# A gated feed-forward after window attention on one core: the first product in a seven-product Strassen form from the sixth chunk on

## The chip, the cores and the metric

The kernel runs on one core of one Trainium2 chip. The metric is the device time of one execution in microseconds; smaller is better. Five engines work side by side, each with its own queue of instructions in a fixed order: PE (TensorE, the matmuls, with weight loads shown as PEld), DVE (VectorE), ACT (ScalarE), POOL (GpSimd), and SP, whose queue issues all transfers. Semaphores tie them together.

## The reference

Sliding-window attention over 8 batches, 8 heads, 576 positions with heads of 64, then a feed-forward with a gate on all 4608 tokens:

```python
scores = scale * np.matmul(q, k.transpose(0, 1, 3, 2))
mask = (rel >= 0) & (rel < window)          # rel = query - key, window = 64
scores = np.where(mask, scores, -1000000000.0)
attn = softmax(scores)
x = (attn @ v)                              # tokens x 512
h = x @ w_in                                # 512 -> 2048
sp = np.maximum(h, 0.0) + np.log1p(np.exp(-np.abs(h)))
g = h * erf(sp)
out = g @ w_out                             # 2048 -> 512
```

The weights come as 64-bit floats and are rebuilt on the chip to 32 bits and then to pairs of f16 numbers.

## The kernel before

**Tiling.** The 4608 tokens are worked in 36 units of 128 tokens for the attention (`u` in the code) and 18 chunks of 256 tokens for the feed-forward (`c`). Each chunk is split into two halves of the hidden dimension (1024 each); a chunk and a half make one of 36 groups (`g`).

**Precision.** Every f32 operand of a matmul is split into a high f16 and a low f16 part, and a product is made of three matmuls: high by high, high by low, low by high. So `x` becomes `xs[0]`, `xs[1]` (`x_hi`, `x_lo`), and after a transposing transfer (`x_turn`) `xt[0]`, `xt[1]`; the weights are `w1[0]`, `w1[1]` and `w2[0]`, `w2[1]`; the gated hidden values are `ghb`, `glb` (`g_hi`, `g_lo`).

**The first product.** `mm1(g, pc)` (L573) makes one of four pieces of a group's hidden values. A piece is 256 hidden features by 256 tokens: 2 feature blocks, 4 blocks of the 512 input features, 3 terms, so 24 matmuls with 128x128 weights and 256 columns, all into one of two banks of PSUM (`hps`, called hp in the profile). `hidden` (L585) then drains the bank, scaled, into `hb` in SBUF, on ACT or DVE. The next piece but one needs that bank again.

**The gate.** On each half of a group (128x1024), ACT makes softplus and erf (L593, L597; each change of function costs a table load), DVE multiplies (`gate`, L601), ACT or DVE casts to gh (`g_hi`), DVE makes gl (`g_lo`, L327 in `rest`). `yb` holds four halves.

**The second product.** `mm2` (L610) makes 16 matmuls of 512 columns with gh (`mA`) and 8 with gl (`mB`) for each half of a group, into two banks `ops`. `result` drains them into `ob`, `store` sends it out.

**The order.** There is no scheduler at work: a long string `PLAN` lists tokens such as `mm:30:1`, `ev:30:1:v` or `gh:29:1:a` (name, numbers, engine letter), and a loop calls the handler of each in turn. The order of the tokens is the order on every engine, the queue SP included. The engine letter says who does a pass: `a` ACT, `v` DVE, `g` POOL. The tokens of the attention of a later chunk (`s` scores, `m` masked maximum, `f` shift, `e` exponential, `a` weighting, `n` normalizing) stand between those of the feed-forward of an earlier one. The listing of the changed kernel numbers its lines anew: `product` is L673 there, `add` L689, the copy in `take` L472 on ACT and L474 on DVE, `mm2` L730.

Of the kernel before, what the change touches and what calls it, by code (L numbers as in the profile page):

```python
# [702 lines left out]
```

## Time and profile before

| | |
|---|---|
| time, median of 3 runs | 900.38 us (898.97 to 901.08) |
| the profiled execution | 900.86 us, its span 899.0 us |
| first product, L581 | 3456 matmuls of 256 columns |
| second product, L617 | 1728 matmuls of 512 columns |
| HBM read, written | 59.44 MB, 9.44 MB |
| largest part of the chain that ended last | PE, 68% |

In the lines of the profile the numbers after a bar are the busy time, the mean duration of one instruction in ns, and then the idle time of the engine just before these instructions with what ended it. A matmul's duration runs from its entry to its last result, and neighbours overlap; how fast matmuls follow each other is read from their start times.

### The profile page before, as it was taken

Reading aid. Unit: us, or ns where it says so; the run is one execution under the profiler, and the core shown is the slowest. Engines: PE = TensorE matmul, PEld = TensorE weight load, DVE = VectorE, ACT = ScalarE, POOL = GpSimd, SP = SyncE. Lnnn points to the kernel's source line nnn. Section 1 sums busy time; section 2 is a strip of 40 time slices with the busy share of each in tenths; the row PEclk is TensorE's granted clock in tenths of the full one; section 3 lists DMA queues with packets and bytes.
Section 4 is the critical chain, followed back from the end, with each engine's and each line's share of the span. In section 5 each row is a group of like instructions: output and inputs, shape, how many; then the busy total and the mean of one; then the engine's idle time right before and its main releaser. Section 6 shows DMA issues by size and latency. Waiting matters only on the chain.

```text
span 899.0 us, 21735 instructions
## 1 busy us (share of the span) xinstructions
PE 866.0 (96%) x9025; PEld 588.4 (65%) x9025; DVE 707.7 (79%) x1594; ACT 701.9 (78%) x814; POOL 192.4 (21%) x195
## 2 busy tenths in 40 slices
...
GB/s 359 305 203 139 203 184 120 71 153 42 51 97 134 131 126 59 137 84 135 89 121 98 141 91 106 65 89 113 118 107 95 63 106 57 49 48 42 7 24 23
DMA packets 140530, 98.59 MB, mean 110 GB/s; under 512 B 117776, under 2 KB 117904, under 8 KB 140432
## 3 DMA queue, kind: packets, MB, share of 16 engines
...
HBM read 59.44 MB, written 9.44 MB: 77 GB/s over the span
## 4 chain that ended last, share of the span: by engine, by line
PE 68%; ACT 13%; DVE 8%; DMA 8%; issue 2%; SPq 0%; POOL 0%; ACTq 0%; DVEq 0%; POOLq 0%
PE o L617 34%; PE hp L581 30%; DMA qr<-q_in 4%; PE av L434 2%; PE s L399 2%; DMA vr<-v_in 2%; ACT L597 1%; ACT y L597 1%; ACT y L593 1%; ACT sm L417 1%; ACT h L320 1%; ACT L593 1%; ACT gh L320 1%; ACT junk L345 1%; ACT L417 1%
## 5 line engine op out<-in xcount | busy, mean ns | idle before, releaser
L581 PE MATMUL hp<-xt,w 128*128 128x256 f16 x3456 | 396.2, 273 | 3.6 <-ACT h L320 1.7
L581 PEld LDWEIGHTS <-w 128*128 128x128 f16 x3456 | 335.9, 98 | 64.0 <-issue 5.3
L617 PE MATMUL o<-w,gh 128*128 128x512 f16 x1152 | 260.6, 379 | 2.9 <-ACT gh L320 2.2
L617 PEld LDWEIGHTS <-gh 128*128 128x128 f16 x1152 | 110.7, 98 | 126.6 <-ACT gh L320 2.7
L617 PE MATMUL o<-w,gl 128*128 128x512 f16 x576 | 136.2, 379 | 0.0
L601 DVE TENSOR_TENSOR y<-h,y 128x1024 f32<-128x1024 f32 x72 | 92.1, 1282 | 38.6 <-ACT y L597 38.3
L320 ACT ACTIVATE h<-hp,c 128x512 f32<-128x512 f32 x85 | 57.6, 678 | 68.7 <-PE hp L581 61.9
L327 DVE SCALAR_TENSOR_TENSOR gl<-y,sg,gh 128x1024 f16<-128x1024 f32 x72 | 94.0, 1307 | 16.6 <-PE o L617 7.9
L593 ACT ACT_TABLE_LOAD x68 | 87.2, 1283 | 21.5 <-DVE h L322 16.9
L617 PEld LDWEIGHTS <-gl 128*128 128x128 f16 x576 | 54.8, 98 | 55.5
L597 ACT ACT_TABLE_LOAD x68 | 87.2, 1283 | 1.2
L413 POOL TENSOR_TENSOR sm<-sm,mx 128x512 f32<-128x512 f32 x41 | 51.3, 1257 | 172.2 <-DVE mx L408 144.2
L593 ACT ACTIVATE y<-h 128x1024 f32<-128x1024 f32 x72 | 75.9, 1056 | 9.6 <-DVE h L322 8.9
L597 ACT ACTIVATE y<-y 128x1024 f32<-128x1024 f32 x72 | 75.9, 1057 | 0.8
L322 DVE TENSOR_SCALAR h<-hp,c 128x512 f32<-128x512 f32 x59 | 43.9, 745 | 40.1 <-PE hp L581 39.2
L408 DVE CUSTOM_DVE_ANT_0 sm<-s,mask 128x128 f32<-128x128 f32 x288 | 64.6, 284 | 7.1 <-PE s L399 6.7
L417 ACT ACTIVATE sm<-sm,shift,cde 128x512 f32<-128x512 f32 x72 | 57.2, 810 | 13.5 <-POOL sm L413 9.4
L320 ACT ACTIVATE gh<-y,sg 128x1024 f16<-128x1024 f32 x44 | 50.0, 1139 | 16.6 <-DVE y L601 8.5
L424 POOL TENSOR_TENSOR p<-sm,p 128x512 f16<-128x512 f32 x32 | 42.5, 1330 | 52.2 <-ACT p L449 29.0
L327 DVE SCALAR_TENSOR_TENSOR vs<-vr,csc,vs 128x1024 f16<-128x1024 f32 x36 | 48.7, 1355 | 1.0 <-ACT vs L320 0.8
L459 POOL TENSOR_TENSOR xs<-x,xs 128x512 f16<-128x512 f32 x17 | 27.0, 1586 | 104.6 <-DVE xs L451 69.0
L417 ACT ACT_TABLE_LOAD x36 | 46.2, 1283 | 0.6
...
## 6 DMA issues: line engine op xcount, KB each, us to landing
...
```

What stands on the lines that cost most here:

```text
L320: nc.scalar.activation(dst, src, AF.Copy, scale=s)
L322: nc.vector.tensor_scalar(dst, src, s, None, op0=ALU.mult)
L327: nc.vector.scalar_tensor_tensor(dst, src, s, hi, op0=ALU.mult, op1=ALU.subtract)
L408: nc.vector.tensor_tensor_reduce(smi(u, par)[:, j, :], sps[par][:, j, :], mask[:, var, :], 1.0, LOWEST, op0=ALU.add, op1=ALU.max, accum_ou ...
L413: eng_of(eng).tensor_tensor(s, s, m.unsqueeze(2).broadcast_to([P, HP, P]), op=ALU.subtract)
L417: nc.scalar.activation(s, s, AF.Exp, bias=shift14, scale=es)
L424: eng_of(eng).tensor_tensor(pp[1][u % 2][:, sl, :], smi(u, par), pp[0][u % 2][:, sl, :], op=ALU.subtract)
L581: nc.tensor.matmul(hps[pc % 2][:, f, :], w1[a][:, cc, fs], xt[b][c % 2][:, cc, :], start=(n == 0), stop=(n == 3 * NCC - 1))
L593: nc.scalar.activation(at(yb, g, n), at(hb, g, n), AF.Softplus)
L597: nc.scalar.activation(y, y, AF.Erf)
L601: nc.vector.tensor_tensor(y, at(hb, g, n), y, op=ALU.mult)
L617: nc.tensor.matmul(ops[j], a[:, f, ts], w2[b][:, hf * GF + f, :], start=f == 0 and a is gh and b == 0, stop=f == GF - 1 and a is gl)
```

## The change

From the sixth chunk on (`FAST = 5`, groups 10 to 35) the four pieces of a group's first product are replaced by seven products in a seven-product form of Strassen's algorithm. The two halves that a matrix is cut into are: the 512 input features in two of 256, the hidden features of a 512-wide block in two of 256, and the 256 tokens in two of 128. A product is `product(g, m)`: 24 matmuls with 128x128 weights and 128 columns. Three products start a bank, four add to what a bank holds; between them the banks are copied into `hb` (`take`, four times) or added to what is there (`add`, three times, on DVE).

The sums of weights that the form needs are made once on the chip, in f32 in `tmp`, and split into two f16 parts (`w_sums`, tokens `S`); they live in three tiles `stage` that held raw weights before, and the fourth sum overwrites a block of `w1`. The sums of x are made for each chunk (`x_sums`, tokens `xd`) in `xo`, so the second unit of a chunk splits and transposes 1280 columns instead of 512.

Scaling moves: `hb` is no longer scaled when drained; softplus takes a scale, the gate multiplies by one, and from the sixth chunk on gh and gl are a plain cast and a plain subtraction, so that gl may run on POOL. `yb` holds three halves instead of four. The string `PLAN` is new as a whole; softplus and erf stand more often in pairs in it.

On PE, the end of one piece and the start of the next in a late group of the kernel before (`w_0` and `w_1` are the high and low parts of w_in, `xt` the transposed x, `hp` the two banks, `gh` with `o` is the second product):

```order
L617 MATMUL o_156<-w_1_140,gh 128x512
L581 LDWEIGHTS w_0_137
L581 MATMUL hp_153<-xt_0_133,w_0_137 128x256
L581 LDWEIGHTS w_0_137
L581 MATMUL hp_153<-xt_0_135,w_0_137 128x256
L581 LDWEIGHTS w_1_138
L581 MATMUL hp_153<-xt_0_133,w_1_138 128x256
```

The same engine in the changed kernel, where the second product of group 33 ends and the sixth begins (`stage` holds sums of weights):

```order
L673 MATMUL hp_155<-xt_0_134,w_0_136 128x128
L673 LDWEIGHTS w_1_137
L673 MATMUL hp_155<-xt_0_132,w_1_137 128x128
L673 LDWEIGHTS stage_149
L673 MATMUL hp_154<-xt_0_132,stage_149 128x128 [waits Activation_49]
L673 LDWEIGHTS stage_149
L673 MATMUL hp_154<-xt_0_134,stage_149 128x128
```

Each matmul has half the columns and still its own weight load, and a product that adds to a bank waits for ACT, which copied the bank out.

On DVE, the last stretch of the kernel before (`h` is `hb`, `c` its scale, `y` is `yb`, `ob` the result):

```order
L322 TENSOR_SCALAR h_142<-hp_153,c_89 128x512 [waits PE_49,Activation_49]
L601 TENSOR_TENSOR y_144<-h_142,y_144 128x1024 [waits Activation_49]
L322 TENSOR_SCALAR gh<-y_144,sg 128x1024 [waits DVE_49]
L327 SCALAR_TENSOR_TENSOR gl<-y_144,sg,gh 128x1024 [waits DVE_49]
L322 TENSOR_SCALAR ob_147<-o_155,sg 128x512 [waits DMAHW6_49,PE_49]
L601 TENSOR_TENSOR y_144<-h_142,y_144 128x1024 [waits Activation_49]
```

And in the changed one, some ten rows from its end:

```order
L689 TENSOR_TENSOR h_140<-hp_155,h_140 128x2x2x128 [waits DVE_49,PE_49]
L721 TENSOR_TENSOR gl<-y_143,gh 128x1024 [waits Activation_49]
L689 TENSOR_TENSOR h_140<-hp_154,h_140 128x2x2x128 [waits Activation_49]
L689 TENSOR_TENSOR h_140<-hp_155,h_140 128x2x2x128 [waits PE_49]
L689 TENSOR_TENSOR h_141<-hp_155,h_141 128x2x2x128 [waits PE_49,Activation_49]
L707 SCALAR_TENSOR_TENSOR y_142<-h_140,cy,y_142 128x1024 [waits DVE_49,Activation_49]
```

The additions of a bank into h stand between the gate and the low parts, on the engine that also releases both.

On POOL, the last rows of the changed kernel, where the kernel before ends with the low part of the last unit of x:

```order
L721 TENSOR_TENSOR gl<-y_142,gh 128x1024 [waits PE_49,Activation_49]
L482 TENSOR_TENSOR x<-x 128x256 [waits DVE_49]
L476 TENSOR_SCALAR gh<-y_143 128x1024 [waits DVE_49,PE_49]
L721 TENSOR_TENSOR gl<-y_143,gh 128x1024 [waits PE_49,Pool_49]
L476 TENSOR_SCALAR gh<-y_142 128x1024 [waits DVE_49,PE_49,Pool_49]
L721 TENSOR_TENSOR gl<-y_142,gh 128x1024 [waits PE_49,Pool_49]
```

Half of all gl and 17 of the gh are POOL's now, and PE's `mB` waits for that engine.

The diff, cut to its core (of the plan two lines near its end):

```diff
-SLOTS = "S0 S1 A B h1 y1 S0 S1 A B S0 S1 S0 S1 S0 S1".split()
+SLOTS = "S0 S1 A B h1 S3 S0 S1 A B S0 S1 S0 S1 S0 S1".split()
+FAST = 5
...
-    "mm:34:1 fo:32:0:a fo:32:1:v gl:33:1 mA:33:0 ev:34:1:a sp:34:0 mm:34:3 er:34:0 gt:34:0 mB:33:0 ev:34:3:a "
+    "ew:33:0:a st:15:0 mw:33:6 xw:33:0 er:32:0 mw:33:5 ew:33:1:a gt:32:0 mw:33:7 ew:33:2:a gh:32:0:g er:32:1 "
...
-    yb = ring("y", 2, [P, GE])
+    yb = ring("y", 3, [P, HE])
...
-    stage = ring("stage", 2, [P, GE])
+    stage = ring("stage", 3, [P, GE])
+    wsum = [t.bitcast(F16).rearrange("p (b c f) -> p b c f", b=2, c=2) for t in stage]
...
+    def x_sums(c, i, eng):
+        dst, a, b = ((xo[:, 4:6, :], xo[:, 2:4, :], xo[:, 0:3:2, :]),
+                     (xo[:, 6, :], xo[:, 3, :], xo[:, 4, :]),
+                     (xo[:, 7, :], xo[:, 1, :], xo[:, 6, :]))[i]
+        eng_of(eng).tensor_tensor(dst, a, b, op=ALU.subtract)
+
+    def x_part(u):
+        j = u % TPC
+        lo, hi = (0, 2) if j == 0 else (2, 4) if u // TPC < FAST else (3, 8)
...
     def hidden(g, pc, eng):
         hv = hb[g % 2].rearrange("p (f t) -> p f t", t=CT)
-        scaled(eng, hv[:, 2 * pc:2 * pc + 2, :], hps[pc % 2], st_c[g][:, pc // 2:pc // 2 + 1])
+        narrow(eng, hv[:, 2 * pc:2 * pc + 2, :], hps[pc % 2])
...
+    def w_sums(j, i, eng):
+        st = WSTEPS[i]
+        if len(st) == 1:
+            narrow(eng, w_blocks(st[0], 0, j), tw)
+        elif len(st) == 2:
+            eng_of(eng).tensor_tensor(w_blocks(st[0], 1, j), tw, w_blocks(st[0], 0, j), op=ALU.subtract)
+        else:
+            a = w_blocks(st[0], 0, j) if st[0] else tw
+            b = w_blocks(st[1][1:], st[2], j) if st[1][1:] else tw
+            eng_of(eng).tensor_tensor(tw, a, b, op=ALU.subtract if st[1][0] == "-" else ALU.add)
+
+    PRODUCTS = {1: (0, 1, "A11", 0), 2: (1, 1, "A12", 2), 3: (1, 0, "S4", 4), 4: (0, 0, "A22", 12),
+                5: (1, 1, "S1", 6), 6: (0, 0, "S2", 10), 7: (0, 0, "S3", 8)}
+
+    def product(g, m):
+        c, hf = ORDER[g]
+        bank, first, name, blk = PRODUCTS[m]
+        for n in range(2):
+            for k in range(2):
+                at = (2 * n + k) * P
+                dst = hps[bank].rearrange("p f t -> p (f t)")[:, at:at + P]
+                for cc in range(2):
+                    for a, b in ((0, 0), (0, 1), (1, 0)):
+                        w = w_block(name, a, 2 * hf + n, cc)[:, k * P:(k + 1) * P]
+                        nc.tensor.matmul(dst, w, xt[b][c % 2][:, blk + cc, :],
+                                         start=bool(first) and at + cc + a + b == 0,
+                                         stop=at + cc + a == 3 * P + 2, skip_group_check=True)
...
+    def take(g, i, eng):
+        narrow(eng, corner(g, (0, 1, 3, 2)[i]), bank_of((0, 0, 1, 0)[i]))
+
+    def add(g, i):
+        dst = corner(g, (0, 3, 1)[i])
+        nc.vector.tensor_tensor(dst, bank_of((1, 0, 1)[i]), dst, op=ALU.add)
...
-        nc.scalar.activation(at(yb, g, n), at(hb, g, n), AF.Softplus)
+        nc.scalar.activation(yat(g, n), at(hb, g, n), AF.Softplus, scale=st_c[g][:, n:n + 1])
...
-    def g_lo(g, n):
+    def g_lo(g, n, eng="v"):
         sl = slice(n * HE, (n + 1) * HE)
-        rest(glb[:, sl], at(yb, g, n), st_g[g][:, n:n + 1], ghb[:, sl])
+        if ORDER[g][0] < FAST:
+            rest(glb[:, sl], yat(g, n), st_s[g][:, n:n + 1], ghb[:, sl])
+        else:
+            eng_of(eng).tensor_tensor(glb[:, sl], yat(g, n), ghb[:, sl], op=ALU.subtract)
```

More of the change, by code (lines that the diff above doesn't have):

```diff
@@ L256, in window_attention_gated_ffn @@
     junk = fixed("junk", [P, HP, P], mybir.dt.uint8)
-    unit = fixed("unit", [P, P])
-    minus = fixed("minus", [P, P], F16)
-    diag = ring("diag", 2, [P, P])
-    st_c, st_g = (cells(n, NG, 3) for n in ("c1", "sg"))
+    tmp = fixed("tmp", [P, 4 * P])
+    diag = [tmp[:, i * P:(i + 1) * P] for i in range(2)]
+    unit, minus = tmp[:, 2 * P:3 * P], tmp[:, 3 * P:].bitcast(F16)[:, :P]
+    st_c, st_g = cells("c1", NG, 2), cells("sg", NG, 1)
+    st_y, st_s = cells("cy", 2, 2), cells("sy", 2 * FAST, 2)
     rmx = ring("mx", 4, [P, HP])
@@ L273, in window_attention_gated_ffn @@
     pt = [ring(f"pt{n}_", 2, [P, H, P], F16) for n in range(2)]
-    xo = ring("x", 1, [P, HP, 2, D])
-    xs = [ring(f"xs{n}_", 2, [P, DM], F16) for n in range(2)]
-    xt = [ring(f"xt{n}_", 2, [P, NCC, CT], F16) for n in range(2)]
+    xo = fixed("x", [P, XSLOTS, CT])
+    xs = [[fixed(f"xs{n}_{i}", [P, (2, 5)[i] * CT], F16) for i in range(2)] for n in range(2)]
+    xt = [ring(f"xt{n}_", 2, [P, XBLOCKS, P], F16) for n in range(2)]
     w1 = ring("w1_", 2, [P, NCC, DF], F16)
@@ L438, in normalize @@
         de, rd = den[u % 2], rde[u % 2]
-        nc.vector.tensor_scalar(de, avp[:, :, :, D:D + 1], 1e-9 * 2.0 ** 14, None, op0=ALU.add)
+        nc.vector.tensor_scalar(de, avp[:, :, :, D:D + 1], 1e-9 * 2.0 ** 14, 4.0, op0=ALU.add, op1=ALU.mult)
         nc.vector.reciprocal(rd, de)
-        nc.vector.tensor_tensor(xo[u % len(xo)].rearrange("p i a d -> p a i d"), avp[:, :, :, :D], rd.broadcast_to([P, 2, HP, D]),
-                                op=ALU.mult)
-    def x_flat(u):
-        return xo[u % len(xo)].rearrange("p i a d -> p (i a d)")
+        x = xo[:, u % TPC * 2:u % TPC * 2 + 2, :].rearrange("p n (i a d) -> p a (n i) d", i=2, a=2)
+        nc.vector.tensor_tensor(x, avp[:, :, :, :D], rd.broadcast_to([P, 2, HP, D]), op=ALU.mult)
     def narrow(eng, dst, src):
@@ L453, in narrow @@
             nc.gpsimd.tensor_scalar(dst, src, 1.0, 1.0, op0=ALU.mult, op1=ALU.mult)
+    def x_sums(c, i, eng):
[6 more added lines that the diff above has]
+        lo, hi = (0, 2) if j == 0 else (2, 4) if u // TPC < FAST else (3, 8)
+        return xo[:, lo:hi, :].rearrange("p n t -> p (n t)"), [s[j][:, :(hi - lo) * CT] for s in xs], slice(4 * j, 4 * j + 2 * (hi - lo))
     def x_hi(u, eng):
-        narrow(eng, xs[0][u % 2], x_flat(u))
+        x, s, _ = x_part(u)
+        narrow(eng, s[0], x)
     def x_lo(u, eng):
-        eng_of(eng).tensor_tensor(xs[1][u % 2], x_flat(u), xs[0][u % 2], op=ALU.subtract)
+        x, s, _ = x_part(u)
+        eng_of(eng).tensor_tensor(s[1], x, s[0], op=ALU.subtract)
     def x_turn(u, n):
-        c, j = divmod(u, TPC)
-        nc.sync.dma_start_transpose(out=xt[n][c % 2][:, :, j * P:(j + 1) * P], in_=xs[n][u % 2])
-    slots = {"h0": hb[0], "h1": hb[1], "y0": yb[0], "y1": yb[1], "S0": stage[0], "S1": stage[1]}
+        _, s, blocks = x_part(u)
+        nc.sync.dma_start_transpose(out=xt[n][u // TPC % 2][:, blocks, :], in_=s[n])
+    slots = {"h0": hb[0], "h1": hb[1], "S0": stage[0], "S1": stage[1], "S3": stage[2]}
     slots = {n: t.bitcast(I32) for n, t in slots.items()}
@@ L518, in pair_scale @@
         exponent(kw, wall)
-        inverse_pow2(sw, kw, 14)
+        inverse_pow2(sw, kw, 12 if j < 4 else 14)
     def pair_diag(j):
@@ L580, in mm1 @@
                 for a, b in ((0, 0), (0, 1), (1, 0)):
-                    nc.tensor.matmul(hps[pc % 2][:, f, :], w1[a][:, cc, fs], xt[b][c % 2][:, cc, :], start=(n == 0),
+                    nc.tensor.matmul(hps[pc % 2][:, f, :], w1[a][:, cc, fs], xt[b][c % 2][:, cc:cc + 5:4, :], start=(n == 0),
                                      stop=(n == 3 * NCC - 1))
@@ L586, in hidden, with w_block @@
         hv = hb[g % 2].rearrange("p (f t) -> p f t", t=CT)
-        scaled(eng, hv[:, 2 * pc:2 * pc + 2, :], hps[pc % 2], st_c[g][:, pc // 2:pc // 2 + 1])
+        narrow(eng, hv[:, 2 * pc:2 * pc + 2, :], hps[pc % 2])
+    def w_block(name, b, j, cc):
+        if name[0] == "S":
+            if name == "S4":
+                return w1[b][:, cc, 512 * j + CT:512 * (j + 1)]
+            return wsum[int(name[1]) - 1][:, b, cc, CT * j:CT * (j + 1)]
+        f0 = 512 * j + CT * (name[1] == "2")
+        return w1[b][:, cc + 2 * (name[2] == "2"), f0:f0 + CT]
@@ new lines, in w_blocks @@
+    def w_blocks(name, b, j):
+        if name[0] == "S" and name != "S4":
+            return wsum[int(name[1]) - 1][:, b, :, CT * j:CT * (j + 1)]
+        f0 = 512 * j + CT * (name == "S4" or name[1] == "2")
+        c0 = 0 if name == "S4" else 2 * (name[2] == "2")
+        return w1[b][:, c0:c0 + 2, f0:f0 + CT]
+    tw = tmp.rearrange("p (c f) -> p c f", c=2)
+    WSTEPS = (("A11", "-A21", 0), ("", "+A11", 1), ("", "-A21", 1), ("S3",), ("S3", 0),
[3 rows of a table added]
+    def w_sums(j, i, eng):
[8 more added lines that the diff above has]
+            eng_of(eng).tensor_tensor(tw, a, b, op=ALU.subtract if st[1][0] == "-" else ALU.add)
@@ new lines, in corner, with bank_of @@
+    def corner(g, i):
+        h = hb[g % 2].rearrange("p (n r k j t) -> p n r k j t", n=2, r=2, k=2, j=2)
+        return h[:, :, i // 2, :, i % 2, :]
+    def bank_of(i):
+        return hps[i].rearrange("p f t -> p (f t)").rearrange("p (n k t) -> p n k t", n=2, k=2)
+    def take(g, i, eng):
[3 more added lines that the diff above has]
+        nc.vector.tensor_tensor(dst, bank_of((1, 0, 1)[i]), dst, op=ALU.add)
@@ L589, in at, with yat @@
     def at(buf, g, n):
         return buf[g % 2][:, n * HE:(n + 1) * HE]
+    def yat(g, n):
+        return yb[(2 * g + n) % 3]
     def softplus(g, n):
-        nc.scalar.activation(at(yb, g, n), at(hb, g, n), AF.Softplus)
+        nc.scalar.activation(yat(g, n), at(hb, g, n), AF.Softplus, scale=st_c[g][:, n:n + 1])
     def erf(g, n):
-        y = at(yb, g, n)
+        y = yat(g, n)
         nc.scalar.activation(y, y, AF.Erf)
     def gate(g, n):
-        y = at(yb, g, n)
-        nc.vector.tensor_tensor(y, at(hb, g, n), y, op=ALU.mult)
+        y, (c, hf) = yat(g, n), ORDER[g]
+        s = (st_c[g] if c < FAST else st_y[hf])[:, n:n + 1]
+        nc.vector.scalar_tensor_tensor(y, at(hb, g, n), s, y, op0=ALU.mult, op1=ALU.mult)
@@ L603, in g_hi @@
     def g_hi(g, n, eng):
-        scaled(eng, ghb[:, n * HE:(n + 1) * HE], at(yb, g, n), st_g[g][:, n:n + 1])
-    def g_lo(g, n):
+        gh = ghb[:, n * HE:(n + 1) * HE]
+        if ORDER[g][0] < FAST:
+            scaled(eng, gh, yat(g, n), st_s[g][:, n:n + 1])
+        else:
+            narrow(eng, gh, yat(g, n))
+    def g_lo(g, n, eng="v"):
         sl = slice(n * HE, (n + 1) * HE)
-        rest(glb[:, sl], at(yb, g, n), st_g[g][:, n:n + 1], ghb[:, sl])
+        if ORDER[g][0] < FAST:
+            rest(glb[:, sl], yat(g, n), st_s[g][:, n:n + 1], ghb[:, sl])
+        else:
+            eng_of(eng).tensor_tensor(glb[:, sl], yat(g, n), ghb[:, sl], op=ALU.subtract)
```

16 lines of the change are left out of this document (10 added, 6 removed), and 359 rows, old and new, of tables (PLAN, WSTEPS).

## The prediction

> **What bounds the kernel now.** I read the page's totals first, then the busy time by stretch, then who PE waited for. On the page: engine, busy time, share, instructions; then the dearest group of matmuls (count, busy time, mean ns of one, idle before).
>
> ```profile
> span 899.0 us, 21735 instructions
> ...
> PE 866.0 (96%) x9025; PEld 588.4 (65%) x9025; DVE 707.7 (79%) x1594; ACT 701.9 (78%) x814; POOL 192.4 (21%) x195
> ...
> L581 PE MATMUL hp<-xt,w 128*128 128x256 f16 x3456 | 396.2, 273 | 3.6 <-ACT h L320 1.7
> ```
>
> PE is busy 96% of the span; the first product (L581) is its largest group. The mean of one (273 ns) is a latency of overlapping matmuls, not a pace. The windows show where the idle 33 us lie (stretch, its length, busy time of each engine, clock, DMA share, GB/s):
>
> ```profile
> 0.00:100.00 100.00, 79.56 (x996) 55.17 (x997) 87.30 (x216) 86.90 (x124) 21.95 (x37) 0.93 0.79 253
> 100.00:300.00 200.00, 195.79 (x2031) 130.19 (x2031) 170.31 (x398) 165.24 (x203) 34.45 (x36) 1.00 0.45 111
> 300.00:785.00 485.00, 480.49 (x5205) 333.23 (x5203) 403.56 (x930) 392.56 (x434) 131.48 (x119) 1.00 0.42 99
> 785.00:899.00 114.00, 110.20 (x797) 69.82 (x794) 46.56 (x55) 57.18 (x56) 4.53 (x4) 1.00 0.12 29
> ```
>
> Columns after the length are PE, PEld, DVE, ACT, POOL. The first 100 us cost PE 20 us; from 300 to 785 us it is idle 4.5 us in 485 while DVE has 83%. The sixth chunk's first product starts near 300 us, so nearly all that the change touches lies where PE alone sets the pace: PE time saved there is saved from the end, unless a new wait appears. PE's waits for the banks of the first product, over the whole run (waiter, releaser: us, times, longest):
>
> ```profile
> PE hp L581 <- ACT h L320: 1.7, 3, 0.9
> PE hp L581 <- DVE h L322: 1.1, 1, 1.1
> ```
>
> That is 2.8 us for 36 x 4 = 144 pieces, 0.019 us each: the two banks are drained in time today.
>
> **Term 1, the matmuls.** In 26 groups (chunks 6 to 18, two halves) 4 pieces of 24 matmuls with 256 columns give way to 7 products of 24 matmuls with 128 columns: 2496 go, 4368 come. First the pace before, from the chain of waits (start, us, what), then nearest rows for short matmuls from PE's timeline, then one line's durations (min/median/max ns):
>
> ```profile
> 200.67 2.62 PE hp L581 x24
> 203.29 1.73 PE o L617 x8
> ```
>
> ```profile
> 8.40 0.22 PE L507 MATMUL av<-ident,acc 128*1 128x128 bf16 x1
> ...
> 30.14 1.95 PE L634 MATMUL hp<-ident 128*128 128x120 bf16 x34
> 32.01 1.14 PE L399 MATMUL s<-ks,qs 64*64 64x128 f16 x48
> 33.08 0.33 PE L507 MATMUL av<-ident,acc 128*1 128x128 bf16 x3
> ```
>
> ```profile
> L634 PEld LDWEIGHTS <-ident x275: 95/98/151, 2.0 to 54.1; 128*128 128x128 bf16 x138
> L634 PE MATMUL hp<-ident x275: 213/216/308, 2.0 to 54.2; 128*128 128x120 bf16 x138
> ```
>
> And the window in which they ran, for that line alone (PE, PEld, clock, DMA):
>
> ```profile
> 30.00:40.00 10.00, 6.23 (x109) 5.75 (x110) 1.00 0.90 323
> ```
>
> One piece takes 2.62 us, 109.2 ns a matmul; removed: 104 x 2.62 = 272.5 us. The clock was full there. No run of matmuls in the trace has 128 columns on full 128x128 weights. L634 is nearest: full weights loaded anew each time, 120 columns, 34 in 1.95 us of which the last takes 0.216: 1.734 / 33 = 52.5 ns apart. Scaled by 128/120 that is 56.0 ns. L507 has 128 columns on a one-column weight: three in 0.33 us, one alone 0.22, so 55 ns apart. Lower bound: half of 109.2, 54.6 ns. Upper bound: L634 with its hand-over, (32.01 - 30.14) / 34 = 55.0, scaled to 58.7 ns. I take 56.0, since L634 alone loads full weights: 4368 x 56.0 = 244.6 us, a saving of **27.9 us**; the bounds give 272.5 - 238.5 = 34.0 and 272.5 - 256.4 = 16.1. So the saving is an eighth of the columns, less what the shorter matmul loses.
>
> **The other engines.** Rows for the added and removed passes (busy, mean ns of one | idle before):
>
> ```profile
> L626 DVE SCALAR_TENSOR_TENSOR ob<-o,sg,ob 128x512 f32<-128x512 f32 x36 | 25.6, 743 | 8.3 <-PE o L617 8.0
> L322 DVE TENSOR_SCALAR h<-hp,c 128x512 f32<-128x512 f32 x59 | 43.9, 745 | 40.1 <-PE hp L581 39.2 <-PE av L366 0.7
> L327 DVE SCALAR_TENSOR_TENSOR gl<-y,sg,gh 128x1024 f16<-128x1024 f32 x72 | 94.0, 1307 | 16.6 <-PE o L617 7.9 <-ACT gh L320 7.4 <-PE av L366 0.6
> L322 DVE TENSOR_SCALAR gh<-y,sg 128x1024 f16<-128x1024 f32 x28 | 22.7, 812 | 15.8 <-PE o L617 15.2
> L413 DVE TENSOR_TENSOR sm<-sm,mx 128x512 f32<-128x512 f32 x31 | 24.1, 781 | 0.4
> L424 DVE TENSOR_TENSOR p<-sm,p 128x512 f16<-128x512 f32 x40 | 31.3, 786 | 2.3 <-POOL p L453 1.4 <-ACT p L449 0.4
> L451 DVE CAST p<-sm 128x512 f16<-128x512 f32 x23 | 11.4, 496 | 0.3 <-ACT sm L417 0.3
> L413 POOL TENSOR_TENSOR sm<-sm,mx 128x512 f32<-128x512 f32 x41 | 51.3, 1257 | 172.2 <-DVE mx L408 144.2 <-DVE den L439 25.7 <-ACT junk L345 2.2
> L424 POOL TENSOR_TENSOR p<-sm,p 128x512 f16<-128x512 f32 x32 | 42.5, 1330 | 52.2 <-ACT p L449 29.0 <-DVE p L451 11.7 <-DVE cmx L354 5.3
> L459 POOL TENSOR_TENSOR xs<-x,xs 128x512 f16<-128x512 f32 x17 | 27.0, 1586 | 104.6 <-DVE xs L451 69.0 <-ACT xs L449 26.8 <-issue 8.7
> L453 POOL TENSOR_SCALAR p<-sm 128x512 f16<-128x512 f32 x24 | 18.0, 752 | 49.8 <-ACT sm L417 42.7 <-DMA vr<-v_in 7.1
> L320 ACT ACTIVATE h<-hp,c 128x512 f32<-128x512 f32 x85 | 57.6, 678 | 68.7 <-PE hp L581 61.9 <-DVE gl L327 5.6 <-PE av L366 0.7
> L593 ACT ACT_TABLE_LOAD x68 | 87.2, 1283 | 21.5 <-DVE h L322 16.9 <-DVE gl L327 3.4
> ```
>
> **DVE:** 78 additions of a bank into h at 0.743 (L626 also reads a bank and SBUF), +58.0; the weights' sums, 22 two-operand passes at 0.781, 9 at 0.786 and 3 casts at 0.496, +25.8; 20 sums of x, 6 of 512 columns and 14 of 256, 6 x 0.781 + 14 x 0.39 = +10.1; plain bank drains 59 to 45, -10.4; gl 72 to 36, -47.1; gh 28 to 12, -13.0. Net +23.4, about 731 us. **POOL:** 36 gl, by twice the L424 row 2.66 each, +95.8; 17 gh at 1.50, +25.6; weights' sums 17 x 1.257 + 7 x 1.330 + 3 x 0.752 = +32.9; x sums 7 x 1.257 + 11 x 0.63 = +15.7. Net +170, about 362 us. **ACT:** table loads 178 to 116, -62 x 1.283 = -79.5; 61 more activations, at 0.678, +41; net -38. All three stay off the bound on average (83%, 41% and 75% of 884), so none enters the sum as busy time; the cover is PE's own 95%. If DVE's cover goes, the second rival below has the price.
>
> **Term 2, before the sixth chunk.** The weights' sums run before the first new product, where DVE is idle 29.7 us of 200 and ACT 34.8. Their 25.8 us on DVE just fit. Nothing lost is one bound, all 25.8 the other; I take **+3**, near the lower one, because POOL takes nearly half of the sums and PE's idle in that window is only 4.2 us with DVE at 85%.
>
> **Term 3, the banks.** A group now hands over a bank 7 times, not 4: four copies (`take`) and three additions (`add`, DVE only), each product waiting for the previous drain of its bank. Behind a drain queued on ACT stand table loads, softplus and erf; behind one on DVE the gate and the softmax; the second product's reads of gh and gl come next on PE. Softplus also has three half-size y buffers instead of four, so it can wait for gl on POOL, and the ACT drains behind it with it. Transposes of x grow from 4 to 10 blocks on SP for the second half of a chunk; the loads behind them are early. Nearest row: 182 products x 0.019 = 3.5 us. Upper bound: each of the 26 groups stands one drain of 0.745, 19.4 us. I take **+5**.
>
> **Term 4, POOL against DVE.** Three lines, one of them on both engines, min/median/max ns:
>
> ```profile
> L413 POOL TENSOR_TENSOR sm<-sm,mx x41: 1038/1040/2127, 35.3 to 778.8; 128x512 f32<-128x512 f32 x41
> L413 DVE TENSOR_TENSOR sm<-sm,mx x31: 669/691/1647, 71.0 to 784.5; 128x512 f32<-128x512 f32 x31
> L424 DVE TENSOR_TENSOR p<-sm,p x40: 672/688/1642, 40.7 to 786.1; 128x512 f16<-128x512 f32 x40
> L327 DVE SCALAR_TENSOR_TENSOR gl<-y,sg,gh x72: 1264/1277/2256, 89.8 to 887.5; 128x1024 f16<-128x1024 f32 x72
> ```
>
> Passes with two SBUF operands mostly take their median, and some about 960 ns more, on either engine, near one pass of the other: one waits the other out. On DVE the excess of mean over median is 90 ns x 31 on L413, 98 x 40 on L424 and 30 x 72 on gl, 8.9 us; the gate and the low parts of q, k and v are about as many passes again, so 18 is my estimate for all. POOL's two-operand time goes from 121 us (L413, L424, L459) to about 280, so the excess may grow 2.3 times, +23 us of DVE time. DVE has that much slack: lower bound 0, upper 23; I take **+3**, on the lower side because PE stayed full from 300 to 785 with DVE at 83%. The Trainium skill, "SBUF — State Buffer", section "Who interferes with whom", says that a VectorE pass with two SBUF inputs and a GpSimd pass exclude each other for a whole instruction. The maxima above agree, and by that rule the 36 long gl on POOL, not their share, decide: the second rival.
>
> **Sum.** -27.9 + 3 + 5 + 3 = -16.9. The profiled execution took 900.86 us (span 899.0 and 1.9 around it), half a microsecond above the median of 900.38. 900.86 - 16.9 = **884 us**.
>
> **Rivals.**
> 1. *The whole saving.* Drains, sums and locks stay covered: 900.9 - 27.9 = 873. For it: 2.8 us of bank waits in 144 pieces, and ACT loses 38 us of work. Against: seven drains on the same two banks, and 66 of the 104 copies stand in ACT's queue with its table loads.
> 2. *POOL's gl blocks DVE, and DVE becomes the bound* between chunk 6 and the end of attention. DVE has 403.6 of 485 us there; without the weights' sums its net is -2, so 402, in a stretch of 485 - 27.9 x 20/26 = 464. If every gl on POOL (2.66 us) stops a DVE pass for all its length, 36 x 2.66 = 96 make 498, 34 over: 873 + 8 + 34 = 915, slower. It decides from (464 - 402) / 36 = 1.7 us of block per gl. For it: the maxima above. Against: collisions are the exception in their groups (medians near the minima).
> 3. *The weight load sets the pace.* Every 128-column matmul needs its own load, which lasts 98 ns in its row. Were they not overlapped, 4368 x 98 = 428 us instead of 272.5: 1056 us. It turns to a loss at 272.5 / 4368 = 62.4 ns. Against it stands L634, which loads full weights each time and runs at 52.5 ns.
>
> The Trainium skill, "TensorE: Matmul & The Clock Gate", section "Back-to-back issue gap", speaks against this change: a sustained stream of load and matmul pairs of 128 columns goes at about 81 ns each. By that, an estimate of 4368 x 81 = 354 us, 81 more than before, 982. The trace's 52.5 ns for 120 columns does not agree.
> That the change doesn't do what it says is excluded: all 4368 matmuls of 128 columns stand in the listing, and 960 of 256.
>
> **How the numbers follow.** Forecast 60% (own range 878 to 892), whole saving 22%, POOL's lock 12% (its partial form ends near no change, 4 of the 12, and 2 still faster), weight load 3%, slower by a cause not seen 3%. The range cuts some 5% below, beyond the 34.0 us bound with nothing added (867), and the slower cases above: 869 to 903. Faster by over 0.2% (below about 898.6, about what a measurement of this kernel can tell): 60 + 22 + 2 = 84%; within it 4%; slower 12%.
>
> **What would show it.** Term 1: a product of 24 should take 1.34 us in the chain; 1.5 or more means the weight load counts. Term 3: PE's waits for hp by ACT and DVE should sum to some 5 us. Term 4: DVE's gate or low-part passes with maxima over 2.5 us, and PE waiting for gl or gh, would show the lock. Term 2: PE idle between 100 and 300 us should stay under 8. A DVE busy over 95% in the middle would make the forecast wrong, and so would a lower granted clock.

## The result and the profile after

| | before | changed |
|---|---|---|
| time, median of 4 runs each | 899.67 us (897.81 to 901.08) | 890.49 us (887.59 to 892.23) |
| ratio, 95% interval | | 0.9896, 0.9862 to 0.9930 |
| the profiled execution | 900.86 us, span 899.0 | 889.82 us, span 888.0 |

The changed kernel is faster by 9.2 us in the medians and by 11.0 in the two profiled executions. The forecast was 16.9, the time of 884 lay 6.5 us too low. Three executions of 1728 us and more, one of the kernel before and one each of runs 2 and 11, are left out of all medians below. First the page of the changed kernel: engine totals, then its groups (count | busy, mean ns of one | idle before).

```profile
span 888.0 us, 25679 instructions
...
PE 845.5 (95%) x10915; PEld 594.2 (67%) x10915; DVE 760.8 (86%) x1623; ACT 656.9 (74%) x810; POOL 348.4 (39%) x276
...
L673 PE MATMUL hp<-xt,w 128*128 128x128 f16 x2496 | 154.8, 220 | 6.4 <-DVE h L689 4.0
...
L673 PE MATMUL hp<-xt,stage 128*128 128x128 f16 x1872 | 113.8, 219 | 4.1 <-DMA xt<-xs 2.4
...
L721 POOL TENSOR_TENSOR gl<-y,gh 128x1024 f16<-128x1024 f32 x36 | 82.0, 2283 | 71.9 <-DVE gh L474 34.3
...
L689 DVE TENSOR_TENSOR h<-hp,h 128x512 f32<-128x512 f32 x78 | 53.1, 683 | 20.0 <-PE hp L673 13.1
```

PE's busy time fell by 20.5 us, yet its idle time rose from 33.0 to 42.5. DVE came out 30 us busier than forecast (731), though each addition took 683 ns, not 743. Where the idle time is, the windows tell (length, PE, PEld, DVE, ACT, POOL, clock, DMA, GB/s; the last bound is moved by the 9 us that were saved up to it):

```profile
0.00:100.00 100.00, 83.05 (x1023) 57.59 (x1024) 87.04 (x226) 88.02 (x125) 27.41 (x43) 0.93 0.82 256
100.00:300.00 200.00, 190.38 (x1973) 127.97 (x1971) 183.94 (x392) 174.62 (x217) 64.07 (x55) 0.99 0.42 105
300.00:776.00 476.00, 463.97 (x6789) 335.32 (x6788) 431.80 (x933) 342.29 (x416) 232.68 (x164) 1.00 0.51 113
776.00:888.00 112.00, 108.13 (x1137) 73.38 (x1134) 58.02 (x79) 51.95 (x55) 24.25 (x15) 1.00 0.13 31
```

PE now idles 12.0 us of 476 in the middle (4.5 of 485 before), and 9.6 from 100 to 300 us (4.2 before). On the chain that ended last PE's share fell from 68% to 49% and DVE's rose from 8% to 25%. The waits of PE by stretch (waiter, releaser: us, times, longest), first 300 to 785 us, then below 300:

```profile
PE hp L673 <- DVE h L689: 4.5, 5, 1.2
PE hp L673 <- DVE h L474: 3.3, 3, 2.4
PE hp L673 <- DMA xt<-xs: 2.4, 4, 1.6
...
PE hp L620 <- ACT ks L346: 3.7, 1, 3.7
...
PE hp L620 <- DMA xt<-xs: 2.1, 2, 1.9
```

Before, the waits for a bank were 2.8 us in the whole run, 1.1 of it on DVE; now DVE alone makes the products wait 7.8 us in the middle. The fourth row is one wait at 134 us; what on ACT it stands for, run 7 asks.

An account by start times adds what idle shares miss. Each matmul with 128x128 weights of 16 bits is given its undisturbed pace (128 columns 56.0 ns, 256 109.2, 512 215.8, 120 53), and what its interval to the next matmul has beyond that is counted as excess; the smaller matmuls of the attention are left out:

| excess over the pace, us | 0 to 100 | 100 to 300 | 300 to 785 | after | sum |
|---|---|---|---|---|---|
| before | 10.5 | 4.0 | 7.6 | 0.4 | 22.5 |
| changed | 13.4 | 6.8 | 16.9 | 0.4 | 37.5 |

At their paces the products save 28.0 us; 15.0 of it comes back as excess, and some 2 through 18 more warm-up matmuls and the small rest: 28 - 17 = 11, the difference of the spans.

**One gap from end to end.** The timeline of the changed kernel around 420 us (start, duration, engine, line, tile; in brackets the idle time before), POOL, DVE and PE:

```profile
415.47 4.40 POOL L721 TENSOR_TENSOR gl<-y,gh 128x1024 f16<-128x1024 f32 x2 [4.64 <-DVE gh L474]
...
415.54 2.35 DVE L474 CAST p<-sm 128x512 f16<-128x512 f32 x1 [0.23 <-ACT sm L443]
417.92 2.50 DVE L450 TENSOR_TENSOR p<-sm,p 128x512 f16<-128x512 f32 x1
420.35 1.40 DVE L739 SCALAR_TENSOR_TENSOR ob<-o,sg,ob 128x512 f32<-128x512 f32 x2
421.67 0.68 DVE L450 TENSOR_TENSOR p<-sm,p 128x512 f16<-128x512 f32 x1
422.26 0.68 DVE L474 COPY h<-hp 128x512 f32<-128x512 f32 x1
...
419.65 0.96 PE L460 MATMUL av<-vs,pt 128*64 128x65 f16 x48
423.00 1.23 PE L673 MATMUL hp<-xt,w 128*128 128x128 f16 x18 [2.39 <-DVE h L474]
```

POOL makes two low parts from 415.47 to 419.87. A cast on DVE begins 0.07 us into the first and is done just after it, a subtraction begins in the second and is done 0.55 us after it: 4.85 us for two passes that otherwise take about 1.1. The copy of the bank (L474) stands behind them in DVE's queue, and PE waits 2.39 us. This is the lock of which the prediction and the experiments speak: a pass on one of the two engines waits until one on the other has ended. The usual durations stand in the views of these lines (count, min/median/max ns):

```profile
L474 DVE CAST p<-sm x18: 407/448/2347, 38.7 to 766.2; 128x512 f16<-128x512 f32 x18
L450 DVE TENSOR_TENSOR p<-sm,p x40: 676/689/2617, 39.1 to 767.1; 128x512 f16<-128x512 f32 x40
L341 DVE TENSOR_SCALAR csc<-cpw x18: 169/170/2137, 26.4 to 742.9; 128x3 int32<-128x3 int32 x18
L707 DVE SCALAR_TENSOR_TENSOR y<-h,cy,y x52: 1262/1280/3171, 328.7 to 869.9; 128x1024 f32<-128x1024 f32 x52
L689 DVE TENSOR_TENSOR h<-hp,h x78: 671/682/692, 305.2 to 862.1; 128x512 f32<-128x512 f32 x78
L721 POOL TENSOR_TENSOR gl<-y,gh x36: 2123/2135/3106, 344.3 to 872.5; 128x1024 f16<-128x1024 f32 x36
```

Even L341, three columns and 0.17 us, once took 2.14, and a gate (L707) took 3.17 instead of 1.28. The additions (L689), which read one bank and one SBUF tile, never took longer. DVE passes lengthened beside one on POOL stand before every gap of 0.55 us or more that PE has behind a drain on DVE from 300 to 785 us. Summed over DVE, time above the usual (each kind's lower quartile) was 33 us before and is 83 now; 33.6 of it lies in 23 passes beside gl on POOL, 1.46 us each. In neither kernel was a DVE pass longer than usual by 0.2 us or more without a pass on POOL beside it.

The wait also has an aftermath. PE's granted clock in the stretches around it (length, busy, clock, DMA, GB/s):

```profile
418.00:423.60 5.60, 3.21 (x124) 1.00 0.30 77
423.60:427.00 3.40, 3.40 (x39) 0.55 1.11 138
427.00:430.00 3.00, 3.00 (x18) 0.94 0.65 228
...
134.00:137.40 3.40, 2.91 (x15) 0.52 0.19 46
```

For some 3.4 us the clock was about half, which adds 1.7 us of excess to the 2.39; the same stands beside the end of the 3.7 us wait at 134 us. The middle's growth of 9.3 us is then: drains on DVE +6.7 (7.8 - 1.1), transposed x +2.4, clock +1.7, and -1.9 for waits that went (the second product's wait for gh among them), 8.9 in all.

### The profile page after: what moved, and what is told of

Same layout as the page of the kernel before. It is cut to its first block, busy times and chain, and to the rows that moved or that the text cites. A ratio compares the mean times of both kernels' runs of the same rounds, so it can differ in the third digit from the quotient of the medians.

```text
span 888.0 us, 25679 instructions
## 1 busy us (share of the span) xinstructions
PE 845.5 (95%) x10915; PEld 594.2 (67%) x10915; DVE 760.8 (86%) x1623; ACT 656.9 (74%) x810; POOL 348.4 (39%) x276
## 4 chain that ended last, share of the span: by engine, by line
PE 49%; DVE 25%; ACT 13%; DMA 5%; issue 5%; POOL 4%; SPq 0%; DVEq 0%; POOLq 0%; ACTq 0%
PE o L730 23%; PE hp L673 16%; PE hp L620 5%; ACT y L698 3%; DVE y L707 2%; DVE sm L434 2%; ACT L698 2%; DVE vs L353 2%; DVE h L689 2%; DVE p L450 2%; PE av L460 1%; ACT y L702 1%; PE s L425 1%; ACT L702 1%; DMA w<-w_in 1%
## 5 line engine op out<-in xcount | busy, mean ns | idle before, releaser
L673 PEld LDWEIGHTS <-w 128*128 128x128 f16 x2496 | 146.4, 98 | 22.8 <-issue 8.9
L673 PE MATMUL hp<-xt,w 128*128 128x128 f16 x2496 | 154.8, 220 | 6.4 <-DVE h L689 4.0
L620 PE MATMUL hp<-xt,w 128*128 128x256 f16 x960 | 113.1, 277 | 6.7 <-ACT ks L346 3.7
L673 PE MATMUL hp<-xt,stage 128*128 128x128 f16 x1872 | 113.8, 219 | 4.1 <-DMA xt<-xs 2.4
L673 PEld LDWEIGHTS <-stage 128*128 128x128 f16 x1872 | 108.0, 98 | 13.1 <-issue 5.8
L721 POOL TENSOR_TENSOR gl<-y,gh 128x1024 f16<-128x1024 f32 x36 | 82.0, 2283 | 71.9 <-DVE gh L474 34.3
L620 PEld LDWEIGHTS <-w 128*128 128x128 f16 x960 | 94.0, 99 | 24.3 <-issue 7.7
L698 ACT ACTIVATE y<-h,c 128x1024 f32<-128x1024 f32 x72 | 79.9, 1143 | 22.5 <-DVE h L474 22.1
L472 ACT ACTIVATE h<-hp 128x512 f32<-128x512 f32 x99 | 57.9, 587 | 51.6 <-PE hp L673 45.0
L707 DVE SCALAR_TENSOR_TENSOR y<-h,cy,y 128x1024 f32<-128x1024 f32 x52 | 70.7, 1378 | 20.2 <-ACT y L702 19.8
L689 DVE TENSOR_TENSOR h<-hp,h 128x512 f32<-128x512 f32 x78 | 53.1, 683 | 20.0 <-PE hp L673 13.1
```

The lines of the kernel that those rows point to most:

```text
L472: nc.scalar.activation(dst, src, AF.Copy)
L620: nc.tensor.matmul(hps[pc % 2][:, f, :], w1[a][:, cc, fs], xt[b][c % 2][:, cc:cc + 5:4, :], start=(n == 0), stop=(n == 3 * NCC - 1))
L673: nc.tensor.matmul(dst, w, xt[b][c % 2][:, blk + cc, :], start=bool(first) and at + cc + a + b == 0, stop=at + cc + a == 3 * P + 2, skip_g ...
L689: nc.vector.tensor_tensor(dst, bank_of((1, 0, 1)[i]), dst, op=ALU.add)
L698: nc.scalar.activation(yat(g, n), at(hb, g, n), AF.Softplus, scale=st_c[g][:, n:n + 1])
L707: nc.vector.scalar_tensor_tensor(y, at(hb, g, n), s, y, op0=ALU.mult, op1=ALU.mult)
```

## The experiments

All times are medians; each set had its own runs of the kernel before, with medians of 899.0 to 900.9. Every kernel is the changed one with the edit shown. Waits, busy times and excess come from one profiled execution of each kernel, so small differences between them are not sure.

| run | time, us | ratio to before, 95% interval |
|---|---|---|
| 1 all gl on DVE | 899.11 | 0.9999, 0.9979 to 1.0018 |
| 2 gl on POOL in quarters | 886.90 | 0.9866, 0.9832 to 0.9901 |
| 3 POOL's gl left out | 882.87 | 0.9810, 0.9792 to 0.9827 |
| 4 all gl on POOL | 896.17 | 0.9960, 0.9940 to 0.9981 |
| 5 bank copies to ACT | 892.48 | 0.9927, 0.9908 to 0.9947 |
| 6 weights' sums left out | 889.56 | 0.9904, 0.9885 to 0.9923 |
| 7 one early drain moved | 892.33 | 0.9925, 0.9910 to 0.9940 |
| 8 three edits at once | 891.70 | 0.9915, 0.9896 to 0.9933 |
| 9 gl on POOL mostly memset | 882.30 | 0.9807, 0.9778 to 0.9835 |
| 10 gl to DVE, 72 passes to ACT | 912.88 | 1.0150, 1.0114 to 1.0186 |
| 11 sums of x to DVE | 893.37 | 0.9937, 0.9916 to 0.9958 |
| 12 some gl in quarters | 887.37 | 0.9838, 0.9809 to 0.9868 |

### 1 to 4: where gl is made, and in what length

Run 1 takes all 36 gl from POOL to DVE:

```diff
-gl:10:1:g gl:11:0:g gl:11:1:g
...
+gl:10:1:v gl:11:0:v gl:11:1:v
...
```

> All 36 low parts gl that POOL makes in the changed kernel (890.5 us) are made on DVE instead, at about 1.22 us each (its free rows). Theory A (POOL's 2.28 us gl passes shut DVE out, so that bank drains on DVE come late): DVE gets 44 us of own work but loses some 30 us of excess over its free durations; the maxima of DVE's two-operand and cast passes fall from over 2.2 to about 1.7 us; time 886 to 893, about as the changed kernel. Theory B (the seven drains on two banks cost it, whatever POOL does): 44 us more on the busiest engine beside PE, time 895 to 905, PE's waits for hp by DVE over 10 us.

The whole gain was lost; the time and the waits for drains on DVE are those that theory B named, and run 3 decides whether its reason holds. PE's largest wait in this kernel:

```profile
PE hp L672 <- DVE h L688: 9.3, 10, 1.9
```

Excess on DVE fell to 54 us, but DVE's own 36 passes (busy 772.7, 12 more) stand in the same queue ahead of the drains. Taking away the lock by giving DVE the work is no gain: run 1 doesn't isolate the lock, it shows that DVE, in this order of passes, has no room for gl.

Run 2 keeps gl on POOL, in four passes of 256 columns:

```diff
-eng_of(eng).tensor_tensor(glb[:, sl], yat(g, n), ghb[:, sl], op=ALU.subtract)
+step = HE if eng == "v" else HE // 4
+for i in range(0, HE, step):
+    o = slice(n * HE + i, n * HE + i + step)
+    eng_of(eng).tensor_tensor(glb[:, o], yat(g, n)[:, i:i + step], ghb[:, o], op=ALU.subtract)
```

> Each gl on POOL is made in four passes of 256 columns instead of one of 1024; nothing else changes. Theory A: DVE can get in between, so a block is at most some 0.7 us; DVE busy falls by 10 to 25 us from 760.8, PE's waits for hp by DVE fall from 7.8 us to about 3; time 882 to 887. Theory B: no gain, POOL itself some 5 to 10 us longer busy; time 889 to 893.

This kernel's waits of PE, then its group on POOL:

```profile
PE hp L673 <- DMA xt<-xs: 5.2, 5, 2.1
...
PE hp L673 <- DVE h L689: 2.3, 4, 1.0
```

```profile
L724 POOL TENSOR_TENSOR gl<-y,gh 128x256 f16<-128x256 f32 x144 | 111.7, 808 | 65.2 <-DVE gh L474 23.7 <-ACT gh L472 23.2 <-PE o L733 16.8
```

Excess beside gl fell from 33.6 to 13.5 us and DVE's waits with it. But 144 quarters keep POOL 111.7 us instead of 82.0; what POOL does for x comes later, and PE waits for the transposed x. The time fell by 3.6 us in the medians, within the range of theory A, but the intervals don't separate it from the changed kernel.

Run 3 leaves POOL's 36 gl out:

```diff
-gl:10:1:g gl:11:0:g gl:11:1:g
...
```

> The 36 gl passes on POOL are left out: those halves multiply an older gl, so the low-by-high term of the second product is not theirs; PE's work is unchanged. Theory A: DVE busy falls by 25 us or more from 760.8, PE's waits for hp by DVE fall below 3 us of 7.8; time 878 to 885. Theory B: bank waits stay over 6 us, time 887 to 892, since seven drains on two banks remain.

882.87, 7.6 us below the changed kernel, with intervals apart. The new products' waits for DVE's drains in this kernel:

```profile
PE hp L668 <- DVE h L684: 0.8, 2, 0.5
...
PE hp L668 <- DVE h L469: 0.3, 1, 0.3
```

1.1 us, as much as PE waited for DVE's drains before the change, with all seven drains a group still there. So theory B, that the drains themselves cost it, falls. Excess in the middle fell from 16.9 to 9.7.

Run 4 goes the other way, and gives POOL the 16 gl that DVE still had from the sixth chunk on:

```diff
-gl:10:0:v gl:13:1:v gl:18:1:v
...
+gl:10:0:g gl:13:1:g gl:18:1:g
...
```

> All 52 gl from the sixth chunk on go to POOL, 16 more than in the changed kernel. Theory A: DVE loses 22 us of own work but is shut out 16 times more, up to 2.3 us each; PE's waits for hp by DVE, and for gl, rise; time 892 to 902. Theory B: DVE is relieved by 22 us, bank waits fall; time 884 to 890.

DVE had 9 us less to do (751.8), and the kernel was 5.7 us slower than the changed one. Its waits of PE for DVE's drains:

```profile
PE hp L672 <- DVE h L688: 5.1, 6, 1.2
PE hp L672 <- DVE h L473: 4.7, 3, 2.4
```

Excess beside gl rose to 43.8 us. So more low parts on POOL cost, though DVE's load falls.

### 5, 10 and 11: is it how much DVE has to do?

Run 5 gives ACT the 37 bank copies that DVE made:

```diff
-ew:11:3:v ew:12:2:v ew:13:2:v
...
+ew:11:3:a ew:12:2:a ew:13:2:a
...
```

> The 37 copies of a bank that DVE makes (take) go to ACT; the 78 additions stay on DVE, POOL's gl is as in the changed kernel (890.5 us). Theory A2 (DVE is all but full between chunk 6 and the end of the attention, by its own passes and by POOL's blocks together, so any 25 us taken from it count): DVE busy falls by some 25 us to 735, PE's waits for hp by DVE from 7.8 to under 4 us, time 882 to 887. Theory B (the banks' drains themselves are too many or too slow): ACT's queue with its table loads drains later, PE waits for hp by ACT instead, 5 us or more, time 889 to 896.

DVE's busy time fell from 760.8 to 734.0, and nothing was gained. PE's waits for drains in this kernel:

```profile
PE hp L672 <- DVE h L688: 8.2, 7, 2.7
...
PE hp L672 <- ACT h L471: 2.0, 4, 1.1
```

27 us less on DVE left the drains as late as ever, and the 5 us of waits for ACT that theory B expected didn't come either. DVE's load as a sum isn't what PE waits for; what stands ahead of an addition when it is due is.

Run 10 takes gl to DVE and gives ACT 72 passes of DVE (bank copies, gh and some of the attention):

```diff
-gl:10:1:g ew:11:3:v ec:13:0:v
...
+gl:10:1:v ew:11:3:a ec:13:0:a
...
```

> All gl on DVE as in the first run, and 72 passes of DVE (37 copies of banks, 16 casts of p, 11 gh, 8 casts of x) moved to ACT. DVE's own work is then about 5 us under the changed kernel's and POOL's gl blocks are gone; ACT has 50 us more, about 710. If DVE's load and blocks are all that is lost: 880 to 886, PE's waits for hp by DVE under 3 us. If ACT's later drains and casts take over, in an order that was not made for it: 888 to 897, waits for hp by ACT and for pt or gh over 5 us.

The slowest of all, outside both forecasts, although DVE (724.2 us) had only 80% of the span and ACT (700.8) 77%. PE's largest waits in it:

```profile
PE hp L672 <- DVE h L688: 11.2, 11, 1.9
PE hp L672 <- ACT h L471: 8.0, 9, 1.6
```

Run 11 makes gl in quarters, the bank copies on ACT, and the sums of x and low parts of x (`xd`, `xl`) on DVE instead of POOL:

```diff
-ew:11:3:v xd:5:1:g xd:5:2:g xl:12:g
...
+ew:11:3:a xd:5:1:v xd:5:2:v xl:12:v
...
```

> Four passes for each gl on POOL, bank copies on ACT, and the x sums and low parts of x from the sixth chunk on moved from POOL to DVE (33 passes). In the run with four passes PE's waits moved from DVE's drains (2.3 us) to the transposed x (5.2 us), since POOL came late with x. If that is so, waits for xt fall under 2.5 us and the time is 882 to 887; if DVE's added 25 us count instead, hp waits by DVE rise over 6 us and the time is 888 to 893.

893.37. PE's waits were ACT's drains 4.5 us, DVE's additions 4.3, transposed x 3.4; neither forecast held, and the run makes three edits at once. Each move put a wait at another place; with two banks and drains in a fixed order, a pass moved to ACT delays drains there.

### 6 and 7: the first 300 us

Run 6 leaves out 39 passes of the weights' sums, 22 on DVE and 17 on POOL, so that the products use weights that are not the sums:

```diff
-S:0:1:g S:0:2:g S:0:5:v
...
```

> 39 of the 40 two-operand passes that form the sums of weights are left out (the casts into the three tiles and the fourth sum's block stay, so products 3, 5, 6 and 7 multiply weights that are no sums); all that comes later is unchanged. Theory C (these sums load DVE and POOL before the sixth chunk, and that is the early loss): about 3 to 6 us less, 884 to 887, PE idle in 100 to 300 us 6 us or less instead of 9.6. Theory D (the early loss is one drain on ACT queued behind the rebias of a late weight tile): nothing, 889 to 892, the 3.7 us wait for hp by ACT stays.

889.56: 0.9 us less, inside the scatter. Excess from 100 to 300 us was 6.7, against 6.8 with the sums. By these profiles, what was lost there the sums' work didn't take.

Run 7 moves one drain on ACT ahead of the weights' work that it stood behind in the 3.7 us wait at 134 us:

```diff
-c:15 d:15
...
-ev:3:3:a
+ev:3:3:a c:15 d:15
...
```

> One token moves: the drain of the last piece of group 3 stands ahead of the rebias of the last weight tile on ACT, not seven ACT passes behind it. Theory D: PE's 3.7 us wait for hp by ACT near 131 us shrinks to under 1, and the half-clock window that follows it near 145 us goes; 2 to 5 us less, 886 to 888. Theory C: under 1 us, since DVE and POOL are as late as before.

The largest wait of PE in this kernel:

```profile
PE hp L619 <- DMA xt<-xs: 6.1, 3, 3.9
```

The wait for ACT went, one of 3.9 us for the transposed x took its place, and the time didn't fall. The drain hid the next thing that was late.

### 8, 9 and 12: the lock by itself, and a version that avoids part of it

Run 8 puts together run 5, run 7 and gl in halves:

```diff
-eng_of(eng).tensor_tensor(glb[:, sl], yat(g, n), ghb[:, sl], op=ALU.subtract)
+step = HE if eng == "v" else HE // 2
...
-ew:11:3:v ew:12:2:v
...
+ew:11:3:a ew:12:2:a
...
-c:15 d:15
...
-ev:3:3:a
+ev:3:3:a c:15 d:15
...
```

> The copies on ACT as in the first run of this set, the early drain moved as in the third, and each gl on POOL in two passes of 512 columns. If A2 and D hold and add up: PE's waits for hp under 4 us in all, time 877 to 883. If B holds: 887 or more.

891.70: waits for transposed x 4.9, for ACT 4.2 early and 1.8 by drains, for DVE 4.1. A miss, as its parts were.

Run 9 keeps POOL as long at work but lets it read little: 32 of 1024 columns are subtracted, the other 992 are set to zero twice, so that the low part of those columns is left out.

```diff
+nc.gpsimd.tensor_tensor(glb[:, o:o + 32], yat(g, n)[:, :32], ghb[:, o:o + 32], op=ALU.subtract)
+for _ in range(2):
+    nc.gpsimd.memset(glb[:, o + 32:o + HE], 0.0)
```

> Each gl on POOL subtracts only its first 32 columns and then sets the other 992 to zero in two memsets, one after the other, which read nothing in SBUF; so POOL is held for about as long and PE waits for the same pass, but for 992 of 1024 columns the low-by-high term of the second product is left out in these halves. Theory A (POOL's reading passes shut DVE out): DVE busy falls by about 30 us from 760.8 as without the gl, DVE's maxima beside gl go, PE's waits for hp by DVE fall below 2 us, time 881 to 885. Theory E (it is POOL's own time: its passes for x, the softmax and gl come later behind 2.1 us each): time 888 to 892, waits for xt and hp as in the changed kernel.

POOL's groups, then PE's waits for DVE's drains, of this kernel:

```profile
L727 POOL MEMSET gl<- 128x992 f16 x72 | 66.9, 929 | 4.1 <-PE o L736 2.0
...
L725 POOL TENSOR_TENSOR gl<-y,gh 128x32 f16<-128x32 f32 x36 | 14.0, 388 | 68.6 <-ACT gh L472 25.6 <-DVE gh L474 25.1 <-PE o L736 16.5
```

```profile
PE hp L673 <- DVE h L689: 0.8, 2, 0.5
...
PE hp L673 <- DVE h L474: 0.4, 2, 0.3
```

A low part took 2 x 0.929 + 0.388 = 2.25 us of POOL, as long as 2.28 in the changed kernel, and POOL was as busy (344.3). Yet the time was 882.30, that of run 3, and excess beside these passes 10.4 us instead of 33.6. POOL's busy time is thus not the price.

What is shows when one takes the DVE passes that began inside a pass on POOL with at least 0.2 us of it left. In the changed kernel 18 with two operands in SBUF began inside a gl, and all 18 were lengthened, by 23.9 us together. In run 9, 19 such passes began inside a memset, and one was lengthened, by 0.25 us. For them the price is that POOL reads. The CAST and TENSOR_SCALAR passes, with one operand to stream, are not freed: six were lengthened inside a gl, by 9.3 us, and nine inside a memset, by 4.9. One of these, on POOL and on DVE:

```profile
482.25 1.91 POOL L727 MEMSET gl<- 128x992 f16 x2
...
483.23 1.20 DVE L348 TENSOR_SCALAR qs<-qr,csc 128x512 f16<-128x512 f32 x1
```

It began with the second memset and ended 0.28 us after it; otherwise it takes 0.48 us. For such passes run 9 only cuts the longest block from 2.13 us to 0.93, and how much of its gain that makes is not separated. PE's waits for the transposed x did not fall: 4.5 us in the middle, 2.4 in the changed kernel.

Another thing isn't separated: memsets don't read y, so its halves come free earlier. Softplus's waits on POOL don't appear among the waits of the changed kernel, which speaks against that as the cause.

Run 12 takes quarters only for the 13 low parts that stood before a gap:

```diff
+short = eng == "g" and (g, n) in {(11, 0), (11, 1), (13, 0), (14, 0), (14, 1), (15, 0), (15, 1), (16, 0), (16, 1), (21, 0), (21, 1), (25, 0), (25, 1)}
+step = HE // 4 if short else HE
```

> Only the 13 low parts on POOL (groups 11, 13 to 16, 21 and 25) beside which the changed kernel's trace showed a lengthened DVE pass ahead of a gap on PE are made in four passes of 256 columns; the other 23 stay whole. Theory A (a long POOL pass that reads two SBUF operands shuts DVE out, and only those that fall ahead of a drain of the banks cost time): 883 to 888 us, PE's waits for hp on DVE fall from 7.8 to under 4 us, POOL's busy time rises by about a third of that of the quarter split of all (about 10 us) and its waits for the transposed x stay under 4 us together. Rival (any shift of the passes only moves the collisions to other groups): 888 to 892 us, and waits for DVE of 5 us or more remain at other places.

PE's waits in this kernel:

```profile
PE hp L673 <- DMA xt<-xs: 4.4, 4, 2.0
...
PE hp L673 <- DVE h L689: 2.2, 5, 0.9
...
PE hp L620 <- DMA xt<-xs: 1.5, 1, 1.5
...
PE hp L673 <- DVE h L474: 0.3, 1, 0.3
```

887.37, with run 2 the fastest that make the whole computation, and not separated from it. As the lock has it, waits on DVE fell from 7.8 to 2.5 us, POOL's busy time rose by 9.7 (358.1). The limit of 4 us for the transposed x was missed, 5.9. After two of these waits, 2.0 us at 439.8 and 1.0 at 474.1, the clock was low (0.57 from 440 to 444 us, 0.74 from 476 to 480), so excess in the middle fell only to 16.0. The gain over the changed kernel, 3.1 us, isn't shown beyond doubt: the intervals of the two ratios touch (0.9809 to 0.9868 and 0.9862 to 0.9930).

## Why the prediction was right, and where its sizes were off

**Term 1, -27.9: right.** The chain of the changed kernel (start, us, what):

```profile
365.51 4.09 PE hp L673 x72
...
488.36 1.34 PE hp L673 x24
...
599.77 4.02 PE hp L673 x72
```

A product of 24 took the forecast 1.34 us, three in a row 4.02: 55.8 ns a matmul. The median from start to start was 56 ns over all 4368. So the weight load, 98 ns each in its group, stays hidden, and the third rival is out.

**Term 2, +3 before the sixth chunk: the size right, the mechanism not.** Excess from 100 to 300 us rose by 2.8, but run 6 without the sums left 6.7 of the 6.8. PE's idle time there, 9.6, also passed the 8 named as the sign. The first 100 us, to which the sum gave nothing, took 2.9 more. Run 7 shows a chain of late things, ACT's drain and then the transposed x. What makes x late is not settled: the plan's order is new there too, and the transposes on SP stand behind weight loads, which wasn't tried. In runs 1, 3 to 5, 9 and 12, whose early part is that of the changed kernel, the excess below 300 us was 19.8 to 23.7 against 14.5 in the one profile of before; the loss stands clear of that spread, but its size is known to some 4 us at best.

**Term 3, +5 for the banks: too large.** With POOL's gl away (runs 3 and 9), PE's waits for DVE's drains are 1.1 and 1.2 us in 182 products, what they were for 144 pieces. Seven drains on two banks cost next to nothing by themselves. What was counted under this term, waits for hp by ACT and DVE of about 5 us, came out at 7.8 in the middle, but through term 4.

**Term 4, +3 for POOL against DVE: too small, the step that failed.** The excess on DVE was forecast to rise by up to 23 us and to be covered mostly by DVE's slack. It rose by 50, from 33 to 83; some 15 of that remain in run 3, beside other passes of POOL. The 18 us from which the prediction started were too low as well, since casts and small TENSOR_SCALAR passes are lengthened too. Runs 3 and 9 put the price of POOL's low parts at 7.6 to 8.2 us of the end. The mistake was to scale the collisions of 512-column passes by POOL's busy time and to set them against a mean share: a block of up to 2.1 us falls on whatever pass is next, and a drain queued behind it keeps PE waiting. Together, terms 3 and 4 were +8 and measured +9.3 in the middle, so the errors of the two nearly cancelled. The sign named for it was half right: the gate reached 3.17 us and a low part of v 2.72, over the 2.5 named, but PE waited for banks, not for gl or gh. The Trainium skill, "SBUF — State Buffer", section "Who interferes with whom", says that a VectorE pass with two SBUF inputs contends only with a GpSimd pass that reads SBUF, not with one that only writes it. Run 9 agrees, with one of 19 such passes lengthened inside a memset against 18 of 18 inside a gl. The prediction had left this condition out; it did not matter for gl, which reads.

**The sum.** -28.0 by pace, +5.7 below 300 us (forecast 3), +9.3 in the middle (8), +2 for warm-up matmuls and small things (0) make -11.0 against -16.9. So of the 5.9 us by which the sum was off, about 2.7 lie below 300 us, where the cause stays open, 1.3 in the middle and 2 in the small things; that the middle came so near is luck. The prediction's counts are each one short for the weights' sums on DVE (23), the sums of x on POOL (19) and the copies on ACT (67), which changes none of this. In the median the gain was 9.2.

**Rivals.** The whole saving, 873, fell by the lock and by the early loss; even run 3 stays at 882.87. POOL's lock as DVE's bound, 915, had the right mechanism at a smaller size: 33.6 us in all, 0.93 for each of 36 gl, under the 1.7 from which it decides; DVE stood at 431.8 of 476 in the middle. Run 4, with 16 more, is the step toward it.
